# Forty-eight chunks of up to 508 tokens instead of fifty-two of up to 470: chunk ends inside stage D's groups

## The chip, the cores and the metric

The kernel runs on one core of one Trainium2 chip. The metric is the device time of one execution in microseconds (us), the median of several runs. One core has TensorE (PE, matrix products), VectorE (DVE), ScalarE (ACT), GpSimd (POOL) and SyncE (SP, which here only issues the transfers). PE takes its weights with a separate load, PEld in the profile.

## The reference

Eight sequences (batches) of 3008 tokens with 256 numbers each go through a transform, a complex mixing matrix, a threshold and the transform back, and the 24,064 tokens that come out go through two matrices with a squared ReLU between them.

```python
X = np.fft.rfft(x, axis=1)
Yr = Xr @ w_r - Xi @ w_i + b_r
Yi = Xr @ w_i + Xi @ w_r + b_i
Yr = np.sign(Yr) * np.maximum(np.abs(Yr) - lam, 0.0)     # Yi alike
y = np.fft.irfft(Y, n=3008, axis=1)
h = np.maximum(y.reshape(24064, 256) @ w_in, 0.0)        # w_in 256 x 2048
return h * h @ w_out                                     # w_out 2048 x 256
```

## The kernel before, in words

**The transform** splits 3008 = 47 x 64. Stage A takes the 47-point part, 64 columns in 13 groups (`GROUPS`: twelve of 5 columns, one of 4). Stage B takes the 64-point part, the mixing, the threshold and the 64-point part back, in 12 pairs of rows (`NPAIR`). Stage D takes the 47-point part back, again in the 13 groups; a group of 5 columns gives 5 x 47 = 235 tokens, the group of 4 gives 188. Between the stages the data go through scratch in HBM (`s1`, `s2`): `store_a` and `load_b`, `store_c` and `load_d`. Nearly every product is done on a high and a low part of each operand, three matmuls each (`mm3`, lines 205 to 207).

**The two matrices** work on chunks of tokens. Before, a chunk is two neighbouring groups of stage D, so it has 470 tokens (48 chunks) or, where the two groups of 4 columns meet at a batch's border, 376 (4 chunks): 52 chunks. Batches with odd numbers begin with their group of 4 columns for this (`groups_of`). A chunk takes 8 rounds (`NU`), 416 rounds in all and 2 more to drain. A round has:

- `mm1`: 12 matmuls of the chunk's full width (470) into `ph`, tokens `xt` by weights `wi`;
- `squares` on ACT (L839 twice, L840): ReLU and square into `g`; `sums` on DVE (L846 to L848): three more combinations of halves, so that seven products of half width do the work of eight;
- one round later the split of `g`: `gh` on ACT (L889) and `gl` on DVE (L897), 7 x 236 = 1652 columns each;
- two rounds later `mm2`: 7 products of three matmuls, 21 of half width (236), into four banks `po`.

After a chunk's last round `put_together` (L864 to L876) adds the products on DVE and issues four stores to `outT`.

**The order is written out by hand.** `plan` holds for each round what of stages A, B and D is issued at fixed places in it: "load" (SP, at the start), "a1" and "a2" (ACT, behind `gh`, and at the end), "p1" (PE, between `mm1` and `mm2`), "p2" (PE, behind `mm2`), "v1" (DVE, behind `gl`, ahead of `sums`) and "v2" (DVE, at the end). Each engine runs its instructions in this order. Call r0 the first round of a batch's stage B. Its pair i is spread over rounds from r0 + 3i: points `psb` at p2 of that round, `psm` (18 matmuls, the mixing) at p1 two rounds on, `psc` at p1 seven rounds on. Stage A's group i has its load in round r0 - 17 + i, its fold (L233, L234, DVE v1) two rounds on, `psa` (6 matmuls, p2) one more on, its store `eva` one or none more on. Stage D's group has its load two rounds ahead of its points `psd` (p1), and the tokens go to `xt` one round on. Batches 0 and 1 do stage A, and batch 0 all, in `start`, ahead of the rounds; so stage B runs in the rounds for batches 1 to 7 and stage A for 2 to 7.

`stage_b` puts r0 of batch 1 at round 2 and each later one 36 + 15 = 51 rounds on, so that stage A of the next batch lies in the 15 rounds between two stages B. Stage D's two groups for a chunk take the last two free rounds (`pair_round`: while stage B runs, only every third) ahead of the chunk.

**Buffers that the change or the steps below touch:** `ps_f`, two PSUM banks that `psa`, `psb`, `psm1`, `psm2`, `psc` and `psd` take in turn; `ld`, two buffers for loads of stages A and B (`xin`, `bin`); `din`, one buffer for loads of stage D; `ev`, two buffers for what goes back to scratch (`eva`, `evc`); `xt`, two chunks of tokens; `ft`, one buffer, used by stage A's fold and by stage B's threshold; `p1`, `o0`, `o1` of `put_together`; `xl` and `z` of stage B.

Of the kernel before, what the change touches and what calls it, by code (L numbers as in the profile page):

```python
# [28 lines left out]
F32 = mybir.dt.float32  # L29
# [15 lines left out]
W = 5  # L45
GROUPS = [(g, min(W, N2 - g)) for g in range(0, N2, W)]
# [118 lines left out]
def fft_mix_moe(ctx: ExitStack, tc: tile.TileContext, xp, xu, w_r, w_i, b_r, b_i,  # L165
                w_in, w_out, t_u, t_a, t_b, t_b0, t_m, t_d, sgn, outT):
    nc = tc.nc
    B = xp.shape[0] + xu.shape[0]
# [85 lines left out]
    def add_e(e, p1, p2):  # L254
        e = e.rearrange("p (c e) -> p c e", c=2)
        nc.vector.tensor_add(e, p1[:, None, 0:D].broadcast_to([P, 2, D]), bias2)
# [11 lines left out]
    def load_d(c, u, t):  # L268
        b, g, w = chunks[c][u]
        nc.sync.dma_start(out=t[:NR * w], in_=scr2[b][:, g:g + w, :])  # L270
# [13 lines left out]
    def unfold(c, u, ps, v, xf):  # L284
        w = chunks[c][u][2]
        n, m = NR * w, N1 * w
        nc.vector.tensor_add(xf[:, :, :n], ps[:, :, 0], v[:, :, :n])
        nc.vector.tensor_sub(xf[:, :, n:m], ps[:, :, 0, w:], v[:, :, w:n])

    def part_x(c, u, xt):  # L290
        m = N1 * chunks[c][u][2]
        base = N1 * sum(w for _, _, w in chunks[c][:u])
        return m, [x[:, :, base:base + m] for x in xt]

    def start():

        with ExitStack() as own:
# [186 lines left out]
            xs, pm, zs, pc, got = {}, {}, {}, {}, {}  # L484
# [50 lines left out]
                copy(i, ev, pc.pop(i))  # L535
                store_c(0, i, ev)

            def inverse(c, xt):
                got = [tl("xl", bufs=2, name="din") for _ in chunks[c]]
                for u, t in enumerate(got):  # L540
                    load_d(c, u, t)
                yield
                for u, t in enumerate(got):
                    ps = points_d(c, u, t, pst("psd"))
                    v = tl("t", name="dv")[:, :2 * NR * W].rearrange("p (k m) -> p k m", k=2)
                    xf = tl("z", name="dx")[:, :2 * N1 * W].rearrange("p (k m) -> p k m", k=2)
                    m, (hi, lo) = part_x(c, u, xt)
                    nc.scalar.copy(v[:, :, :ps.shape[3]], ps[:, :, 1])
                    unfold(c, u, ps, v, xf)
# [16 lines left out]
            xt = alloc_x(0)  # L566
            late = tables_main()
            for n in range(NPAIR + 3):
# [35 lines left out]
    xts = {0: start()}  # L604
# [20 lines left out]
    def at(r, place, do):  # L625
        plan.setdefault((r, place), []).append(do)
# [50 lines left out]
    def plan_b(b, r0):  # L677
        for i in range(NPAIR):
            def steps(i=i):
                s = {}  # L680
# [32 lines left out]
                    add_e(s["e"], *s["p"])  # L713

                def threshold():
                    t = tl("ft", name="t")
                    nc.vector.tensor_scalar(t, s["e"], LAM, -LAM, op0=ALU.min, op1=ALU.max)
                    nc.vector.tensor_sub(s["e"], s["e"], t)

# [27 lines left out]
                r = r0 + PAIR * i  # L747
# [14 lines left out]

            steps()

    def plan_d(c, u, r):
        s = {}

        def load():
            if c not in xts:
                xts[c] = alloc_x(c)  # L770
            s["t"] = tl("din")
            load_d(c, u, s["t"])

        def points():
            s["ps"] = points_d(c, u, s["t"], pst("psd"))

        def take():
            s["v"] = tl("xh", (P, 3, 2, P), name="dv").rearrange("p a b m -> p (a b m)")
            s["v"] = s["v"][:, :2 * NR * W].rearrange("p (k m) -> p k m", k=2)
            nc.scalar.copy(s["v"][:, :, :s["ps"].shape[3]], s["ps"][:, :, 1])  # L780

        def unfolded():
            s["x"] = tl("xl", (P, 3, 2, P), name="dx").rearrange("p a b m -> p (a b m)")
            s["x"] = s["x"][:, :2 * N1 * W].rearrange("p (k m) -> p k m", k=2)
            unfold(c, u, s["ps"], s["v"], s["x"])

        def high():
            m, (hi, lo) = part_x(c, u, xts[c])
            nc.scalar.copy(hi, s["x"][:, :, :m])

        def low():
            m, (hi, lo) = part_x(c, u, xts[c])
            nc.vector.tensor_sub(lo, s["x"][:, :, :m], hi.bitcast(F32))  # L793
# [64 lines left out]
    def put_together(c, po):  # L858
        n = cols[c]
        m, t0 = halves(n)  # L860
        p = {s: po[bank][:, half * m:half * m + m] for s, bank, half in PLACES}
        p1 = tl("p1", (P, HALF))[:, :m]
        o = [tl(f"o{k}", (P, 2, HALF))[:, :, :m] for k in range(2)]
        nc.scalar.copy(p1, p[0])  # L864
        add, sub = nc.vector.tensor_add, nc.vector.tensor_sub
        add(o[0][:, 0], p[2], p1)
# [4 lines left out]
        add(o[0][:, 1], p[3], o[0][:, 1])  # L871
        sub(o[1][:, 0], o[1][:, 0], p[1])
        for k in range(2):
            for t, (a, b) in enumerate(((0, t0), (0, m))):
                to = col0[c] + t * t0
                nc.sync.dma_start(out=outT[k * P:(k + 1) * P, to:to + b - a], in_=o[k][:, t, a:b])  # L876
# [4 lines left out]
    with tc.manual_schedule():  # L881
        for r in range(last + LAG):
            c, j = divmod(r, NU)
            run(r, "load")
            k = r - 1
            if k in hid:
                m, _ = halves(cols[k // NU])
# [6 lines left out]
            if r < last:  # L894
                g = squares(c, ph)
# [7 lines left out]
            k = r - LAG  # L903
# [48 lines left out]
```

## Time and profile before

| | us |
|---|---|
| median of 3 runs | 2704.31 (2702.66 to 2705.11) |
| the profiled execution, its own time | 2704.11 |
| its span in the trace | 2702.3 |
| PE busy | 2624.7 (97% of the span) |
| PE weight loads busy | 2425.5 (90%) |
| DVE busy | 2147.3 (79%) |
| ACT busy | 2031.8 (75%) |
| mean granted TensorE clock | 0.99 |

The page counts a matmul as busy from its start to its modelled end, and neighbours overlap, so PE's busy share is no measure of its pace; the distance between two starts in the timeline is. In a row of a group of instructions stand line, engine, operation, output<-input, shapes, count, then busy us and mean ns of one, then the idle time of the engine ahead of them and who ended it. In a row of the timeline stand start in us, duration in us, engine, line, operation, and in brackets the idle time ahead of it. SPq is SP's issuing of transfers.

### The profile page before, as it was taken

How to read it: one execution, taken by the hardware profiler on the slowest of the kernel's cores; microseconds unless marked ns; L12 is line 12 of the kernel's file. 1: busy time of each engine (PE TensorE's matmuls, PEld its weight loads, DVE VectorE, ACT ScalarE, POOL GpSimd, SP SyncE). 2: the span in 40 equal slices, each digit the busy share in tenths (PEclk: the TensorE clock that was granted, in tenths of full speed). 3: DMA queues.
4: the chain of work that ended last, by engine and by line, in shares of the span. 5: the costliest groups of instructions: out<-in, count | busy, mean ns of one | idle time of the engine just before them, and what ended most of it. 6: DMA issues, size and time to landing. Idle time of an engine off the chain costs nothing.

```text
span 2702.3 us, 44970 instructions
## 1 busy us (share of the span) xinstructions
PE 2624.7 (97%) x17816; PEld 2425.5 (90%) x17816; DVE 2147.3 (79%) x3301; ACT 2031.8 (75%) x2885; POOL 51.3 (2%) x60
## 2 busy tenths in 40 slices
PE   7889999999999999999999999999999999999998
PEld 4579999999899999999989999999999999999997
DVE  4768888788788888888888888878888888777776
ACT  3668787787777778778777877878877787766765
POOL 1410000000000000000000000000000000000000
PEclk8989999999999999999999999999999999999999
DMA  8611113111221112211132112311123121000000
GB/s 253 192 47 53 44 49 101 51 43 54 67 84 49 39 43 85 79 39 52 46 92 62 49 37 60 99 54 47 39 75 94 35 57 35 27 28 25 19 26 19
DMA packets 130068, 165.33 MB, mean 61 GB/s; under 512 B 11440, under 2 KB 92066, under 8 KB 129666
## 3 DMA queue, kind: packets, MB, share of 16 engines
q1 hardware_dynamic: 129858, 162.44, 20.2%
q8 instruction: 142, 2.33, 0.4%
q14 instruction: 68, 0.56, 0.1%
HBM read 87.43 MB, written 74.97 MB: 60 GB/s over the span
## 4 chain that ended last, share of the span: by engine, by line
PE 47%; DVE 26%; ACT 19%; issue 5%; DMA 2%; POOL 1%; SPq 0%; ACTq 0%; DVEq 0%; POOLq 0%
ACT gh L889 10%; DVE gl L897 7%; PE ph L205 6%; PE ph L206 6%; PE ph L207 6%; PE po L207 6%; PE po L206 6%; PE po L205 6%; DVE g L846 4%; ACT g L840 3%; ACT g L839 3%; DVE g L847 3%; DVE g L848 2%; PE psm L207 2%; PE psb L242 2%
## 5 line engine op out<-in xcount | busy, mean ns | idle before, releaser
L897 DVE TENSOR_TENSOR gl<-g,gh 128x1652 fp32r<-128x1652 f32 (+1 forms) x416 | 770.4, 1852 | 345.1 <-ACT gh L889 345.1
L889 ACT CAST gh<-g 128x1652 fp32r<-128x1652 f32 (+1 forms) x416 | 645.9, 1553 | 401.2 <-DVE g L848 320.9
L205 PE MATMUL po<-gh,wo 128*128 128x236 f32 (+1 forms) x2912 | 809.4, 278 | 5.1 <-DVE o L871 1.8
L206 PE MATMUL po<-gl,wo 128*128 128x236 f32 (+1 forms) x2912 | 799.2, 274 | 2.4 <-DVE gl L897 2.4
L207 PE MATMUL po<-gh,wo 128*128 128x236 f32 (+1 forms) x2912 | 799.9, 275 | 0.0
L205 PE MATMUL ph<-xt,wi 128*128 128x470 f32 (+1 forms) x1664 | 634.9, 382 | 16.9 <-ACT xt L199 10.5
L206 PE MATMUL ph<-xt,wi 128*128 128x470 f32 (+1 forms) x1664 | 624.5, 375 | 4.0 <-DVE xt L793 3.7
L207 PE MATMUL ph<-xt,wi 128*128 128x470 f32 (+1 forms) x1664 | 619.2, 372 | 0.0
L205 PEld LDWEIGHTS po<-gh,wo 128*128 128x128 f32 x2912 | 555.3, 191 | 19.1 <-DVE o L871 5.9
L206 PEld LDWEIGHTS po<-gl,wo 128*128 128x128 f32 x2912 | 554.7, 190 | 8.9 <-DVE gl L897 2.8
L207 PEld LDWEIGHTS po<-gh,wo 128*128 128x128 f32 x2912 | 556.4, 191 | 0.0
L839 ACT ACTIVATE g<-ph 128x472 f32<-128x472 f32 (+1 forms) x832 | 417.6, 555 | 66.7 <-PE ph L207 66.5
L840 ACT ACTIVATE g<-g 128x944 f32<-128x944 f32 (+1 forms) x416 | 408.9, 983 | 13.2
L205 PEld LDWEIGHTS ph<-xt,wi 128*128 128x128 f32 x1664 | 315.7, 190 | 52.6 <-ACT xt L199 10.7
L207 PEld LDWEIGHTS ph<-xt,wi 128*128 128x128 f32 x1664 | 314.5, 189 | 39.5
L206 PEld LDWEIGHTS ph<-xt,wi 128*128 128x128 f32 x1664 | 316.6, 190 | 34.8 <-DVE xt L793 6.8
L846 DVE TENSOR_TENSOR g<-g 128x472 f32<-128x472 f32 (+1 forms) x416 | 266.4, 640 | 38.0 <-ACT g L840 26.2
L848 DVE TENSOR_TENSOR g<-g 128x236 f32<-128x236 f32 (+1 forms) x416 | 166.6, 400 | 14.4
L847 DVE TENSOR_TENSOR g<-g 128x236 f32<-128x236 f32 (+1 forms) x416 | 166.5, 400 | 14.3
L207 PE MATMUL psm<-wm,xl 128*128 128x256 f32 (+1 forms) x552 | 162.0, 293 | 4.5 <-DVE xl L702 3.8
L205 PE MATMUL psm<-wm,xh 128*128 128x256 f32 (+1 forms) x552 | 160.9, 291 | 0.0
L206 PE MATMUL psm<-wm,xh 128*128 128x256 f32 (+1 forms) x552 | 159.3, 289 | 0.0
(107 smaller groups left out, 2771.1 us busy)
## 6 DMA issues: line engine op xcount, KB each, us to landing
bin<-s SPq DMA_DIRECT2D x96, 256.0 KB
s<-evc SPq DMA_DIRECT2D x96, 256.0 KB
din<-s SPq DMA_DIRECT2D x96, 240.0 KB
xin<-in_xp_dram SPq DMA_DIRECT2D x72, 240.0 KB
s<-eva SPq DMA_DIRECT2D x72, 240.0 KB
outT_dram<-o SPq DMA_DIRECT2D x96, 118.0 KB
outT_dram<-o SPq DMA_DIRECT2D x96, 117.0 KB
s<-eva SPq DMA_DIRECT2D x22, 192.0 KB
```

The source lines that it names most:

```text
L205: nc.tensor.matmul(out, l0, r0, start=start, stop=False, **kw)
L206: nc.tensor.matmul(out, l0, r1, start=False, stop=False, **kw)
L207: nc.tensor.matmul(out, l1, r0, start=False, stop=stop, **kw)
L242: nc.tensor.matmul(ps[:, k, :, q, :], tv[:, q, k], tB[:, 0:r + 2:r + 1], start=True, stop=True)
L839: nc.scalar.activation(g[:, t:4:2, :m], ph[:, :, t * t0:t * t0 + m], AF.Relu)
L840: nc.scalar.activation(g[:, 0:4, :m], g[:, 0:4, :m], AF.Square)
L846: nc.vector.tensor_sub(g[:, 4:6, :m], g[:, 1:4:2, :m], g[:, 0:2, :m])
L847: nc.vector.tensor_sub(g[:, 6, :m], g[:, 3, :m], g[:, 4, :m])
L848: nc.vector.tensor_sub(g[:, 1, :m], g[:, 6, :m], g[:, 2, :m])
L889: nc.scalar.copy(gg[k][0][:, :, :m], hid[k][:, :, :m])
L897: nc.vector.tensor_sub(gg[k][1][:, :, :m], hid.pop(k)[:, :, :m], gg[k][0][:, :, :m].bitcast(F32))
```

## The change

A batch now has six chunks of 470, 508, 508, 508, 508 and 506 tokens (`WIDTHS`), 48 chunks and 384 rounds in all. `mm1` is up to 508 wide, `mm2` up to 254, `gh` and `gl` 7 x 254 = 1778. All batches take the groups in the same order. Chunk ends lie inside four of a batch's 13 groups: such a group writes its first tokens to the current `xt` as before (round r + 1), and the others, which belong to the chunk after it, stay in `o0`'s buffer until the current chunk's matmuls begin: in that round the `xt` of the chunk before comes free, and they are copied there. These are four more casts on ACT and four more subtractions on DVE in each batch. Stage D's first load of a batch waits for the round `done`, one earlier after the last pair than before. `stage_b` starts at round 3 and repeats every 48 rounds, so the 15 rounds of stage A begin in round r0 + 33 of the batch before. The threshold's scratch is now in `z`, and `p1` in `o1`.

```diff
-def groups_of(b):
-    return GROUPS if b % 2 == 0 else GROUPS[-1:] + GROUPS[:-1]
+WIDTHS = (2 * W * N1, 508, 508, 508, 508, 506)
+NCH = len(WIDTHS)
...
-    HALF = (W * N1 + 1) // 2 * 2
-    NCOL = 2 * W * N1
+    NCOL = max(WIDTHS)
+    HALF = (NCOL // 2 + 1) // 2 * 2
...
-    chunks = [flat[i:i + 2] for i in range(0, len(flat), 2)]
-    cols = [N1 * sum(w for _, _, w in ch) for ch in chunks]
+    nch = NCH * B
+    cols = [WIDTHS[c % NCH] for c in range(nch)]
+    col0 = [sum(cols[:c]) for c in range(nch)]
+    def pieces(b, i):
+        g, w = GROUPS[i]
+        a, z = b * S + N1 * g, b * S + N1 * (g + w)
+        out = []
+        for c in range(NCH * b, NCH * (b + 1)):
+            lo, hi = max(a, col0[c]), min(z, col0[c] + cols[c])
+            if lo < hi:
+                out.append((c, lo - col0[c], hi - lo, lo - a))
+        return out
...
                 def threshold():
-                    t = tl("ft", name="t")
+                    t = tl("z", name="t")
...
         def unfolded():
-            s["x"] = tl("xl", (P, 3, 2, P), name="dx").rearrange("p a b m -> p (a b m)")
+            if len(parts) == 1:
+                x = tl("xl", (P, 3, 2, P), name="dx").rearrange("p a b m -> p (a b m)")
+            else:
+                x = tl("o0", (P, 2, HALF), name="dx").rearrange("p a m -> p (a m)")
...
-        at(r - 2, "load", load)
+        at(max(r - 2, done.get(b, 0)), "load", load)
...
-        at(r + 1, "a1", high)
-        at(r + 1, "v1", low)
+        for k, part in enumerate(parts):
+            q = NU * (part[0] - 1) if k else r + 1
+            at(q, "a1", lambda part=part: high(*part))
+            at(q, "v1", lambda part=part: low(*part))
...
-    stage_b = {1: 2}
-    for b in range(2, B):
-        stage_b[b] = stage_b[b - 1] + PAIR * NPAIR + TURN
-    done = {b: r + PAIR * (NPAIR - 1) + 9 for b, r in stage_b.items()}
+    stage_b = {b: 3 + NU * NCH * (b - 1) for b in range(1, B)}
+    done = {b: r + PAIR * (NPAIR - 1) + 8 for b, r in stage_b.items()}
...
-        for u in (1, 0):
-            r = rounds.pop()
+        units = [i for i in range(len(GROUPS)) if pieces(b, i)[0][0] == c]
+        for i, r in zip(units, rounds[-len(units):]):
...
-        p1 = tl("p1", (P, HALF))[:, :m]
         o = [tl(f"o{k}", (P, 2, HALF))[:, :, :m] for k in range(2)]
+        p1 = o[1][:, 0]
```

Two places show what moves. The first is DVE in round r0 + 35 of batch 2, in which the last pair's mixing is biased. Before, from that pair's `zl` on (names: `e<-psm` takes a mixing bank and frees it, `g` are the sums, `gl` opens the next round):

```order
L735 TENSOR_TENSOR zl<-z,zh 128x512
L846 TENSOR_TENSOR g<-g 128x472
L847 TENSOR_TENSOR g<-g 128x236
L848 TENSOR_TENSOR g<-g 128x236
L256 TENSOR_TENSOR e<-psm_7118,bias_68 128x512
L257 TENSOR_TENSOR e<-psm_7119,e 128x512
L897 TENSOR_TENSOR gl<-g,gh 128x1652
```

and now:

```order
L741 TENSOR_TENSOR zl<-z,zh 128x512
L233 TENSOR_TENSOR f<-xin 120x256
L234 TENSOR_TENSOR f<-xin 120x256
L858 TENSOR_TENSOR g<-g 128x508
L859 TENSOR_TENSOR g<-g 128x254
L860 TENSOR_TENSOR g<-g 128x254
L256 TENSOR_TENSOR e<-psm_7092,bias_68 128x512
L257 TENSOR_TENSOR e<-psm_7093,e 128x512
L659 TENSOR_TENSOR fl<-f,fh 120x512
L909 TENSOR_TENSOR gl<-g,gh 128x1778
```

The next batch's folds `f` now stand ahead of the sums and of the two adds that free the mixing banks, and its `fl` behind them; every width of the two matrices' work is larger.

The second place is SP at the border from batch 2 to 3, from the last stores of stage A (`eva`) to the first loads of stage B (`bin`). Before:

```order
L270 DMA din<-s_2_4635 120x1x512
L226 DMA s_3_7034<-eva 24x5x512
L270 DMA din<-s_2_4635 120x1x512
L226 DMA s_3_7034<-eva 24x5x512 x3
L226 DMA s_3_7034<-eva 24x4x512
L222 DMA bin<-s_3_7034 128x2x256 x2
L270 DMA din<-s_2_4635 120x1x512
```

and now:

```order
L280 DMA din<-s_2_4555 120x1x512
L226 DMA s_3_6771<-eva 24x5x512
L280 DMA din<-s_2_4555 120x1x512
L226 DMA s_3_6771<-eva 24x5x512
L226 DMA s_3_6771<-eva 24x4x512
L888 DMA outT_dram<-o_7932 128x252
L888 DMA outT_dram<-o_7932 128x254
L888 DMA outT_dram<-o_7933 128x252
L888 DMA outT_dram<-o_7933 128x254
L222 DMA bin<-s_3_6771 128x2x256 x2
L280 DMA din<-s_2_4555 120x1x512
```

Four output stores now stand between the last `eva` and the first `bin`, and a second `din`, which needs the points of the first one done, stands ahead of the last two `eva` instead of the last four.

More of the change, by code (lines that the diff above doesn't have):

```diff
@@ L57 @@
 F_MAX = _f32(0x47EFFFFF)
-def groups_of(b):
-    return GROUPS if b % 2 == 0 else GROUPS[-1:] + GROUPS[:-1]
+WIDTHS = (2 * W * N1, 508, 508, 508, 508, 506)
+NCH = len(WIDTHS)
 def token_order(b):
     n1 = np.r_[np.arange(NR), N1 - np.arange(1, NR)]
-    return np.concatenate([((64 * n1[:, None] + 47 * (g + np.arange(w))) % S).reshape(-1) for g, w in groups_of(b)])
+    return np.concatenate([((64 * n1[:, None] + 47 * (g + np.arange(w))) % S).reshape(-1) for g, w in GROUPS])
 def folded_rows():
@@ L257, in add_e, with load_d, points_d @@
         nc.vector.tensor_add(e, p2.rearrange("p (c e) -> p c e", c=2), e)
-    flat = [(b, g, w) for b in range(B) for g, w in groups_of(b)]
-    chunks = [flat[i:i + 2] for i in range(0, len(flat), 2)]
-    cols = [N1 * sum(w for _, _, w in ch) for ch in chunks]
-    col0 = [sum(cols[:c]) for c in range(len(chunks))]
-    nch = len(chunks)
+    nch = NCH * B
+    cols = [WIDTHS[c % NCH] for c in range(nch)]
+    col0 = [sum(cols[:c]) for c in range(nch)]
+    assert sum(WIDTHS) == S
+    def pieces(b, i):
[7 more added lines that the diff above has]
+        return out
     def alloc_x(c):
         return [const.tile([P, 2, NCOL], F32R, tag=f"xt{k}", name=f"xt{k}", bufs=2) for k in range(2)]
-    def load_d(c, u, t):
-        b, g, w = chunks[c][u]
+    def load_d(b, i, t):
+        g, w = GROUPS[i]
         nc.sync.dma_start(out=t[:NR * w], in_=scr2[b][:, g:g + w, :])
-    def points_d(c, u, t, ps):
-        b, g, w = chunks[c][u]
+    def points_d(i, t, ps):
+        g, w = GROUPS[i]
         n = NR * w
@@ L282, in points_d, with unfold @@
         return ps
-    def unfold(c, u, ps, v, xf):
-        w = chunks[c][u][2]
+    def unfold(i, ps, v, xf):
+        w = GROUPS[i][1]
         n, m = NR * w, N1 * w
@@ L288, in unfold @@
         nc.vector.tensor_sub(xf[:, :, n:m], ps[:, :, 0, w:], v[:, :, w:n])
[L290 to L293, printed above, removed]
     def start():
@@ L536, in pair_out, with inverse @@
                 store_c(0, i, ev)
-            def inverse(c, xt):
-                got = [tl("xl", bufs=2, name="din") for _ in chunks[c]]
+            def inverse(xt):
+                got = [tl("xl", bufs=2, name="din") for _ in range(2)]
                 for u, t in enumerate(got):
-                    load_d(c, u, t)
+                    load_d(0, u, t)
                 yield
                 for u, t in enumerate(got):
-                    ps = points_d(c, u, t, pst("psd"))
+                    ps = points_d(u, t, pst("psd"))
                     v = tl("t", name="dv")[:, :2 * NR * W].rearrange("p (k m) -> p k m", k=2)
                     xf = tl("z", name="dx")[:, :2 * N1 * W].rearrange("p (k m) -> p k m", k=2)
-                    m, (hi, lo) = part_x(c, u, xt)
+                    (_, base, m, _), = pieces(0, u)
+                    hi, lo = (x[:, :, base:base + m] for x in xt)
                     nc.scalar.copy(v[:, :, :ps.shape[3]], ps[:, :, 1])
-                    unfold(c, u, ps, v, xf)
+                    unfold(u, ps, v, xf)
                     split(xf[:, :, :m], hi, lo)
@@ L591, in start @@
                     weights()
-            inv = inverse(0, xt)
+            inv = inverse(xt)
             next(inv)
@@ L763, in plan_b, with plan_d @@
             steps()
-    def plan_d(c, u, r):
+    def plan_d(b, i, r):
         s = {}
+        parts = pieces(b, i)
         def load():
-            if c not in xts:
-                xts[c] = alloc_x(c)
             s["t"] = tl("din")
-            load_d(c, u, s["t"])
+            load_d(b, i, s["t"])
         def points():
-            s["ps"] = points_d(c, u, s["t"], pst("psd"))
+            s["ps"] = points_d(i, s["t"], pst("psd"))
         def take():
@@ L782, in unfolded, with high, low @@
         def unfolded():
-            s["x"] = tl("xl", (P, 3, 2, P), name="dx").rearrange("p a b m -> p (a b m)")
[L784 to L793, printed above, removed]
-        at(r - 2, "load", load)
+            if len(parts) == 1:
+                x = tl("xl", (P, 3, 2, P), name="dx").rearrange("p a b m -> p (a b m)")
+            else:
+                x = tl("o0", (P, 2, HALF), name="dx").rearrange("p a m -> p (a m)")
+            s["x"] = x[:, :2 * N1 * W].rearrange("p (k m) -> p k m", k=2)
+            unfold(i, s["ps"], s["v"], s["x"])
+        def high(c, to, m, a):
+            if c not in xts:
+                xts[c] = alloc_x(c)
+            nc.scalar.copy(xts[c][0][:, :, to:to + m], s["x"][:, :, a:a + m])
+        def low(c, to, m, a):
+            hi, lo = (x[:, :, to:to + m] for x in xts[c])
+            nc.vector.tensor_sub(lo, s["x"][:, :, a:a + m], hi.bitcast(F32))
+        at(max(r - 2, done.get(b, 0)), "load", load)
         at(r, "p1", points)
@@ L816, in fft_mix_moe @@
     for c in range(1, nch):
-        rounds = [r for r in range(NU * (c - 1) + 1, NU * c - 1) if pair_round(r)]
-        for u in (1, 0):
-            r = rounds.pop()
-            assert r - 2 >= done.get(chunks[c][u][0], 0) - 2 and r >= 2, (c, u, r)
-            plan_d(c, u, r)
+        b = c // NCH
+        rounds = [r for r in range(max(NU * (c - 1) - 1, 2), NU * c - 1) if pair_round(r)]
+        units = [i for i in range(len(GROUPS)) if pieces(b, i)[0][0] == c]
+        for i, r in zip(units, rounds[-len(units):]):
+            assert r - 1 >= done.get(b, 0), (c, i, r)
+            assert len(pieces(b, i)) == 1 or r >= NU * (c - 1) + 2, (c, i, r)
+            plan_d(b, i, r)
     def mm1(c, j):
```

1 line of the change is left out of this document (removed).

## The prediction

> **What bounds the kernel now.** I read the page's shares first, then the timeline of PE where stage B runs, then the groups by form, then the waits.
>
> ```profile
> PE 2624.7 (97%) x17816; PEld 2425.5 (90%) x17816; DVE 2147.3 (79%) x3301; ACT 2031.8 (75%) x2885; POOL 51.3 (2%) x60
> ```
>
> PE is the fullest engine, but its share says nothing of its pace. The timeline of PE does (start, duration, line, operation); here is the first matmul of each run of one kind, over one round and a half:
>
> ```profile
> 1507.09 0.39 PE L205 MATMUL psc<-zh,tMs 128*128 128x512 f32 x1
> ...
> 1507.78 0.27 PE L205 MATMUL po<-gh,wo 128*128 128x236 f32 x1
> ...
> 1510.13 0.37 PE L205 MATMUL ph<-xt,wi 128*128 128x470 f32 x1
> ...
> 1512.68 0.28 PE L205 MATMUL psm<-wm,xh 128*128 128x256 f32 x1
> ...
> 1514.71 0.28 PE L205 MATMUL po<-gh,wo 128*128 128x236 f32 x1
> ...
> 1517.06 0.38 PE L205 MATMUL ph<-xt,wi 128*128 128x470 f32 x1
> ```
>
> The kernel issues 3 `psc`, 21 `po`, 12 `ph` and 18 `psm` in these runs, so the distances are 0.69/3 = 0.230 us at 512 columns, 2.35/21 = 0.112 at 236, 2.55/12 = 0.2125 at 470 and 2.03/18 = 0.113 at 256. Run follows run without a hole: PE's issue is the bound here. The distances do not grow with the width below 256. A round of a 376 chunk shows it more clearly:
>
> ```profile
> 484.79 0.33 PE L206 MATMUL ph<-xt,wi 128*128 128x376 f32 x1
> ...
> 486.66 0.25 PE L205 MATMUL po<-gh,wo 128*128 128x188 f32 x1
> ...
> 488.98 0.36 PE L205 MATMUL ph<-xt,wi 128*128 128x376 f32 x1
> ```
>
> Eleven `ph` take 1.87, 0.170 each; 21 `po` of 188 columns take 2.32, 0.1105 each, as much as 236 columns. The groups by form say the same of thousands (the mean ns follows the bar):
>
> ```profile
> L205 PE MATMUL po<-gh,wo 128*128 128x236 f32 x2688 | 747.5, 278 | 4.2 <-DVE o L871 1.4 <-DVE o L866 1.1 <-ACT gh L889 0.8
> L206 PE MATMUL ph<-xt,wi 128*128 128x470 f32 x1536 | 581.7, 379 | 3.5 <-DVE xt L793 3.3
> L205 PE MATMUL po<-gh,wo 128*128 128x188 f32 x224 | 61.9, 276 | 0.9 <-DVE o L871 0.4 <-DVE o L866 0.3
> L206 PE MATMUL ph<-xt,wi 128*128 128x376 f32 x128 | 42.8, 334 | 0.4 <-DVE xt L793 0.4
> ```
>
> So `mm1` pays for columns, `mm2` pays by the matmul. The kernel pays 52 x 8 x 21 = 8736 of the latter, and the idle time ahead of these groups is a few us in all.
>
> **The change part by part.** *Fewer, wider matmuls.* A round of a 470 chunk costs PE 12 x 0.2125 + 21 x 0.112 = 4.90, one of a 376 chunk 12 x 0.170 + 21 x 0.1105 = 4.36; before, 384 x 4.90 + 32 x 4.36 = 2021. The new widths have no row, so I bound them. `ph` at 508: the line through 470 and 512 gives 0.2283, the one through 376 and 470 gives 0.2297; I take 0.229. `po` at 254: one neighbour is `psm` at 256 with 0.113, the other is `psa`, also at 256:
>
> ```profile
> 749.15 0.28 PE L205 MATMUL psa<-fh,tAs 120*120 120x256 f32 x1
> ...
> 749.74 0.28 PE L207 MATMUL psa<-fh,tAs 120*120 120x256 f32 x1
> ```
>
> Five steps in 0.59, 0.118 each; less two columns, 0.117. The line through `ph` at 376 and 470, drawn down to 254, gives 0.115, in the middle, and I take that: columns begin to count where they take longer than the floor of 0.111. A new round is then 12 x 0.229 + 21 x 0.115 = 5.16, and 64 x 4.90 + 320 x 5.16 = 1965: **-56**. With `po` at 0.1125 and `ph` at 0.2283 it would be -75, with 0.117 and 0.2297 it would be -39. The matmuls of stages A, B and D keep their number.
>
> *The two element engines.* DVE's part of a round grows as well:
>
> ```profile
> L897 DVE TENSOR_TENSOR gl<-g,gh 128x1652 fp32r<-128x1652 f32 x384 | 721.4, 1879 | 317.6 <-ACT gh L889 317.6
> L846 DVE TENSOR_TENSOR g<-g 128x472 f32<-128x472 f32 x384 | 248.9, 648 | 33.7 <-ACT g L840 23.0
> L848 DVE TENSOR_TENSOR g<-g 128x236 f32<-128x236 f32 x384 | 155.2, 404 | 13.2
> L897 DVE TENSOR_TENSOR gl<-g,gh 128x1316 fp32r<-128x1316 f32 x32 | 48.9, 1529 | 27.5 <-ACT gh L889 27.5
> ```
>
> It is now 1.879 + 0.648 + 2 x 0.404 = 3.34 (L847 as L848); the two forms of `gl` differ by 350 ns over 336 columns, 1.04 ns a column, so 254 wide it is 2.01 + 0.685 + 2 x 0.423 = 3.54. That is 0.20 more in a round in which PE gets 0.26 more: the balance stays, and `gl`'s 317.6 us of waiting for ACT show that DVE has room. The 32 extra casts and 32 extra subtractions of the split groups lie in that room: 0.
>
> *Stage A over the end of stage B.* This is the new place, rounds r0 + 33 to r0 + 36, at six borders. DVE there:
>
> ```profile
> L702 DVE TENSOR_TENSOR xl<-x,xh 128x768 fp32r<-128x768 f32 x84 | 79.9, 952 | 0.0
> L793 DVE TENSOR_TENSOR xt<-dx,xt 128x470 fp32r<-128x470 f32 x94 | 60.5, 643 | 0.0
> L718 DVE TENSOR_TENSOR e<-e,t 128x512 f32<-128x512 f32 x84 | 58.2, 692 | 2.9
> L735 DVE TENSOR_TENSOR zl<-z,zh 128x512 fp32r<-128x512 f32 x84 | 57.5, 685 | 0.0
> L256 DVE TENSOR_TENSOR e<-psm,bias 128x512 f32<-128x512 f32 x84 | 57.4, 684 | 0.0
> L653 DVE TENSOR_TENSOR fl<-f,fh 120x512 fp32r<-120x512 f32 x72 | 49.4, 686 | 10.6 <-ACT fh L649 10.4
> L287 DVE TENSOR_TENSOR dx<-psd,dv 128x240 f32<-128x240 f32 x96 | 38.9, 405 | 50.2 <-ACT dv L780 48.5 <-ACT dv L548 1.7
> L717 DVE TENSOR_SCALAR t<-e 128x512 f32<-128x512 f32 x84 | 35.3, 421 | 0.0
> L250 DVE TENSOR_TENSOR x<-x 128x256 f32<-128x256 f32 x84 | 35.2, 419 | 0.0
> L233 DVE TENSOR_TENSOR f<-xin 120x256 f32<-120x256 f32 x72 | 30.2, 419 | 0.2
> ```
>
> Four rounds at 3.54 are 14.2; two thresholds 2 x 1.11, one sum and low part 1.37, one `zl` 0.69, two biased adds 1.37, one unfolded group with its low part 1.4, four folds with theirs 4 x 1.52 = 6.1: 27.4 in all. PE has 4 x 5.16, `psd` and `psb` (8 each at 0.112) 1.8, `psc` 0.7, `psm` 2.0, three `psa` 2.1: 27.2. So DVE is level with PE for four rounds, and what it was late by is not hidden. One wait is new: in r0 + 35 `psa` needs the bank that the first biased add frees. In the round shown above that add was
>
> ```profile
> 1516.62 0.68 DVE L256 TENSOR_TENSOR e<-psm,bias 128x512 f32<-128x512 f32 x1
> ```
>
> so it ended at 1517.30, 0.24 after PE had gone on to the next round at 1517.06. A fold of 0.84 ahead of it makes that 1.1 us, and `psa` stands in PE's order ahead of the next `mm1`, so all of PE waits. With half as much again for late low parts I take 1.5 us a border, 6 x 1.5 = **+9**; bounds 0 (DVE comes in early) and 4 us a border.
>
> *SP at the border.* The first `bin` needs the last `eva` landed; four output stores now stand between.
>
> ```profile
> 465.94 0.88 SPq L876 DMA_DIRECT2D outT_dram<-o  x2
> ...
> 476.42 1.58 SPq L226 DMA_DIRECT2D s<-eva  x2
> ...
> 480.76 4.41 SPq L222 DMA_DIRECT2D bin<-s  x3
> ...
> 483.65 1.13 PE L242 MATMUL psb<-tB,bin 128*128 128x128 f32 x8 [0.54 <-DVE dx L287]
> ```
>
> Here SP had issued the last `eva` at 478.0 and waited for it until 480.76. Four stores at 0.44 are 1.8 and fit into these 2.8, so `bin` leaves no later. I count 0.3 us a border for their traffic, **+2** (bounds -5 to +12, as the rivals explain). Stage D's first load one round nearer to its points costs 0: `bin` above was used 2.9 us after its issue, and a round is over 5.
>
> *Four `put_together` fewer*, each seven adds of 0.4 on DVE of which PE loses a part: **-2** (0 to -4). `p1` in `o1` and the threshold in `z` find their buffers long free: 0.
>
> The sum: -56 + 9 + 2 - 2 = -47, on 2704.1 of the profiled execution (span 2702.3 and 1.8 around it), which stands 0.2 under the median of the runs: **2657**.
>
> **The rivals.** *The floor still covers 254 columns* (`psm`'s 0.113 speaks for it; `psa`'s 0.118 and the line of `ph` against): -75 + 9 = **2638**. The Trainium skill, TensorE: Matmul & The Clock Gate, sections "LDWEIGHTS (loading the stationary operand)" and "Back-to-back issue gap", would side with it: it has a weight load take columns/1.2 ns, 106.7 for 128, and a warm matmul N/2.4 + 2.5, 108.3 for 254. By its figures alone, an estimate, the matmuls' sum would be -61; the trace has 0.2125 at 470 where that rule has 0.198, so its slope is not this kernel's.
>
> *DVE binds at the borders.* With DVE level with PE, folds that wait for their `xin` (the second one now waits on SP for the last `psb` to free its buffer) make every delay PE's: 5 us a border instead of 1.5, +21, **2678** to 2690. For it speak the sums above, against it that DVE idles for 317.6 us of `gl` alone and enters the border with slack.
>
> *Slower: SP blocked at both ends of a border.* Two groups of stage D in neighbouring rounds share the one `din`: the second load stops SP until the first group's points, and stores behind it keep `ev`. Once, before, that reached PE:
>
> ```profile
> 735.78 0.78 SPq L270 DMA_DIRECT2D din<-s  x1
> ...
> 740.51 0.58 ACT L744 COPY evc<-psc 128x512 f32<-128x512 f32 x1 [4.02 <-DMA s<-eva]
> ...
> 741.14 0.57 PE L205 MATMUL psa<-fh,tAs 120*120 120x256 f32 x1 [3.05 <-ACT evc L744]
> 741.51 0.41 PE L206 MATMUL psa<-fl,tAs 120*120 120x256 f32 x1
> 741.72 0.41 PE L207 MATMUL psa<-fh,tAs 120*120 120x256 f32 x1
> ```
>
> PE lost 3.05 us, and after it ran `psa` at 0.21 instead of 0.118, so some 5 us. Each border now has two such pairs, so at worst 10 to 11 us a border: -58 + 66, **2712**. It decides from 10.5 us a border on. Against it: the other such pair shown above (478 to 484) cost PE 0.54, and `evc` now leaves SP ahead of both `din`. If the one old stall vanishes, that is the -5 in the bounds.
>
> **How the numbers follow.** My forecast 0.62 (its own range 2645 to 2675), the covered floor 0.17, DVE at the borders 0.13, SP 0.04, something unseen 0.04. The range 2634 to 2692 leaves out the SP case and the ends of the others. Over 0.2% (5.4 us, about what a measurement tells from no change) faster: 0.92, within it 0.03, slower 0.05.
>
> **What would show it.** In the profile after: 8064 `po` at about 0.115 between starts and `ph` near 0.229; in rounds r0 + 35 a `psa` waiting about 1 us for DVE's biased add; `bin` issued when the last `eva` has landed. I am wrong if `po` at 254 goes at 0.112 or 0.118, if PE waits over 3 us at a border, or if rounds away from the borders show waits that they did not have.

## The result and the profile after

| | before | after |
|---|---|---|
| median, us | 2703.48 (2700.08 to 2705.11, 4 runs) | 2671.36 (2670.41 to 2673.4, 4 runs) |
| profiled execution, its own time | 2704.11 | 2671.44 |
| its span | 2702.3 | 2669.7 |

The ratio is 0.9885, with a 95% interval of 0.9873 to 0.9898: 32 us less, where 47 were forecast.

The page's shares after (engine, busy us, share of the span, instructions) have PE at 97% as before:

```profile
PE 2583.5 (97%) x16760; PEld 2328.8 (87%) x16760; DVE 2123.1 (80%) x3177; ACT 2014.2 (75%) x2785; POOL 50.9 (2%) x60
```

So again the timeline has to tell the pace. Here is the first matmul of each run of one kind, over two rounds and a half of the kernel after:

```profile
1518.12 0.39 PE L205 MATMUL psc<-zh,tMs 128*128 128x512 f32 x1
...
1518.82 0.28 PE L205 MATMUL po<-gh,wo 128*128 128x254 f32 x1
...
1521.30 0.39 PE L205 MATMUL ph<-xt,wi 128*128 128x508 f32 x1
...
1524.05 0.28 PE L205 MATMUL psm<-wm,xh 128*128 128x256 f32 x1
1526.10 0.28 PE L205 MATMUL po<-gh,wo 128*128 128x254 f32 x1
...
1528.60 0.39 PE L205 MATMUL ph<-xt,wi 128*128 128x508 f32 x1
...
1531.35 0.28 PE L205 MATMUL po<-gh,wo 128*128 128x254 f32 x1
```

Twelve `ph` take 2.75, 0.229 each, as forecast. Twenty-one `po` take 2.48 and 2.50: 0.118 and 0.119 each, where 0.115 was taken and 0.117 was the upper bound.

What PE waited for, by the view of the waits (releaser, us in total, times, longest). Before:

```profile
PE psb L242 <- DMA bin<-s: 16.6, 2, 15.3
...
PE psa L205 <- ACT evc L744: 3.0, 1, 3.0
PE psd L280 <- DMA din<-s: 2.6, 2, 2.4
```

After:

```profile
PE psb L242 <- DMA bin<-s: 19.2, 3, 15.6
PE psd L290 <- DMA din<-s: 11.5, 7, 3.3
...
PE psm L205 <- ACT eva L670: 2.3, 6, 0.4
...
PE psa L205 <- DVE e L256: 1.6, 6, 0.3
```

(In both, the longest wait of `psb` for `bin` and of `psd` for `din` is one at the start, ahead of the rounds.) All rows of this view add to 70.7 us before and to 78.9 after. Three waits are new. One is the forecast one, `psa` for the biased add, once a border; it is 0.3 instead of 1.1. The `psm` just ahead of it waits as well. And `psd` waits for `din` at the borders, which the prediction had put at 0. `psb` waits once at each border too; the view puts four of these six waits down to DVE's sums (3.7 us in all), but they go with the others in `e5_start` below. One border in the timeline, where the four waits shown add to 3.4 us:

```profile
399.75 0.38 PE L205 MATMUL psm<-wm,xh 128*128 128x256 f32 x1 [0.42 <-ACT eva L670]
...
404.19 0.38 PE L205 MATMUL psa<-fh,tAs 120*120 120x256 f32 x1 [0.26 <-DVE e L256]
...
448.42 1.15 PE L290 MATMUL psd<-tD,din 120*128 120x120 f32 x8 [1.52 <-DMA din<-s]
...
489.86 1.13 PE L242 MATMUL psb<-tB,bin 128*128 128x128 f32 x8 [1.19 <-DMA bin<-s]
```

### The profile page after: what moved, and what is told of

Same layout as the page of the kernel before. It is cut to its first block, busy times and chain, and to the rows that moved or that the text cites. A ratio compares the mean times of both kernels' runs of the same rounds, so it can differ in the third digit from the quotient of the medians.

```text
span 2669.7 us, 42564 instructions
## 1 busy us (share of the span) xinstructions
PE 2583.5 (97%) x16760; PEld 2328.8 (87%) x16760; DVE 2123.1 (80%) x3177; ACT 2014.2 (75%) x2785; POOL 50.9 (2%) x60
## 4 chain that ended last, share of the span: by engine, by line
PE 61%; DVE 19%; ACT 12%; DMA 4%; issue 3%; POOL 1%; ACTq 0%; SPq 0%; DVEq 0%; POOLq 0%
PE ph L205 8%; PE ph L206 8%; PE ph L207 8%; PE po L205 7%; PE po L207 7%; PE po L206 7%; ACT gh L901 6%; DVE gl L909 5%; DVE g L858 3%; PE psb L242 3%; PE psm L207 2%; PE psd L290 2%; PE psm L205 2%; PE psm L206 2%; ACT g L852 2%
## 5 line engine op out<-in xcount | busy, mean ns | idle before, releaser
L909 DVE TENSOR_TENSOR gl<-g,gh 128x1778 fp32r<-128x1778 f32 (+1 forms) x384 | 763.6, 1989 | 332.9 <-ACT gh L901 332.9
L901 ACT CAST gh<-g 128x1778 fp32r<-128x1778 f32 (+1 forms) x384 | 638.7, 1663 | 381.7 <-DVE g L860 305.8
L205 PE MATMUL po<-gh,wo 128*128 128x254 f32 (+1 forms) x2688 | 764.8, 285 | 6.4 <-DVE o L878 3.6
L206 PE MATMUL po<-gl,wo 128*128 128x254 f32 (+1 forms) x2688 | 753.0, 280 | 2.6 <-DVE gl L909 2.6
L207 PE MATMUL po<-gh,wo 128*128 128x254 f32 (+1 forms) x2688 | 752.9, 280 | 0.0
L205 PE MATMUL ph<-xt,wi 128*128 128x508 f32 (+2 forms) x1536 | 608.6, 396 | 16.2 <-ACT xt L199 10.6
L206 PE MATMUL ph<-xt,wi 128*128 128x508 f32 (+2 forms) x1536 | 599.9, 391 | 1.8 <-DVE xt L802 1.7
L207 PE MATMUL ph<-xt,wi 128*128 128x508 f32 (+2 forms) x1536 | 599.0, 390 | 0.0
L205 PEld LDWEIGHTS po<-gh,wo 128*128 128x128 f32 x2688 | 509.4, 190 | 21.1 <-DVE o L878 7.7
L207 PEld LDWEIGHTS po<-gh,wo 128*128 128x128 f32 x2688 | 510.4, 190 | 0.0
L851 ACT ACTIVATE g<-ph 128x508 f32<-128x508 f32 (+1 forms) x768 | 410.4, 588 | 68.9 <-PE ph L207 67.7
L852 ACT ACTIVATE g<-g 128x1016 f32<-128x1016 f32 (+1 forms) x384 | 401.5, 1046 | 12.2
L858 DVE TENSOR_TENSOR g<-g 128x508 f32<-128x508 f32 (+1 forms) x384 | 260.7, 679 | 46.1 <-ACT g L852 39.4
L859 DVE TENSOR_TENSOR g<-g 128x254 f32<-128x254 f32 (+1 forms) x384 | 161.6, 421 | 13.2
L860 DVE TENSOR_TENSOR g<-g 128x254 f32<-128x254 f32 (+1 forms) x384 | 161.5, 421 | 13.2
```

The costliest lines, as they stand in the source:

```text
L205: nc.tensor.matmul(out, l0, r0, start=start, stop=False, **kw)
L206: nc.tensor.matmul(out, l0, r1, start=False, stop=False, **kw)
L207: nc.tensor.matmul(out, l1, r0, start=False, stop=stop, **kw)
L851: nc.scalar.activation(g[:, t:4:2, :m], ph[:, :, t * t0:t * t0 + m], AF.Relu)
L852: nc.scalar.activation(g[:, 0:4, :m], g[:, 0:4, :m], AF.Square)
L858: nc.vector.tensor_sub(g[:, 4:6, :m], g[:, 1:4:2, :m], g[:, 0:2, :m])
```

## The experiments

All but `e8_overlap` are edits of the kernel after. Times are set against it by the ratios of both to the kernel before, which ran beside each on the same chip; a ratio is uncertain by about 0.0013, 3.5 us, and a difference of two by about 5.

**The width alone (`e1_narrow`, `e2_ladder`).**

```diff
+        n = m if j == 0 or m < 254 else 240     # e2: 250, 246, 242, 238, 230 by chunk
-            mm3(po[bank][:, half * m:half * m + m], ... (gg[0][:, s, :m], gg[1][:, s, :m]), ...
+            mm3(po[bank][:, half * m:half * m + n], ... (gg[0][:, s, :n], gg[1][:, s, :n]), ...
```

> In every second-layer step but the first of a chunk, the matmuls into po of the 508 chunks take 240 of their 254 columns; the products of the other 14 columns are left out in seven of eight rounds. All else is as in the changed kernel. In its trace po of 254 columns stands 0.1185 us from the next, po of 236 before stood at 0.112. Theory A: beyond the floor the columns are paid for, and 254 is beyond it. 320 rounds x 7/8 x 21 = 5880 matmuls each go back by 0.0065: -38 us, so 2633. Theory B: the spacing rose for something else in the new rounds (more operands in flight, DVE's or ACT's traffic), not for the width: within 5 us of 2671. In between, the width explains that share of 38.

> One look at the curve. The second-layer matmuls of the six chunks of a batch take 236 (the 470 chunk, unchanged), 250, 246, 242, 238 and 230 columns in seven of eight steps; the remaining columns' products are left out there. Theory A (a floor of about 0.112 us, and above it the columns at the slope of the ph rows, some 0.45 ns each): 250 at 0.117, 246 at 0.115, 242 at 0.113, 238 and 230 at 0.112, so the knee lies near 240. Theory B (the floor reaches past 250 and something else slows the 254 round): one value for all widths. Theory C (no floor, all linear): 230 at 0.108 and falling by 0.0018 per four columns.

Measured: `e2_ladder` 2657.2 in its one run. Its timeline, first `po` of a run and the first matmul behind the run, at 250, 242, 238 and 230 columns:

```profile
559.29 0.28 PE L205 MATMUL po<-gh,wo 128*128 128x250 f32 x1
...
561.74 0.39 PE L205 MATMUL ph<-xt,wi 128*128 128x508 f32 x1
...
651.77 0.27 PE L205 MATMUL po<-gh,wo 128*128 128x242 f32 x1
...
654.14 0.39 PE L205 MATMUL ph<-xt,wi 128*128 128x508 f32 x1
...
699.52 0.27 PE L205 MATMUL po<-gh,wo 128*128 128x238 f32 x1
...
701.88 0.39 PE L205 MATMUL ph<-xt,wi 128*128 128x508 f32 x1
...
754.43 0.27 PE L205 MATMUL po<-gh,wo 128*128 128x230 f32 x1
...
756.77 0.28 PE L205 MATMUL psa<-fh,tAs 120*120 120x256 f32 x1
```

By 21 that is 0.1167, 0.1129, 0.1124 and 0.1114 (246 columns lie between, at 0.1152). Theory A holds: a floor of 0.112 up to about 240 columns, and above it some 0.45 ns for each column, the slope of `ph`. Width alone explains the 0.1185 at 254.

`e1_narrow` has its `po` at 0.1125, as expected, which is 35 us less of issue. But it took 2655.69 (2651.34 to 2663.27), ratio 0.9823 (0.9808 to 0.9839): only 17 less. By what was expected, the missing half would be something other than the width; but the distances show that the width gave all 35. Half of it was lost again somewhere else.

**Where the other half went (`e12_light`, `e13_elem`).** `e12_light` narrows ACT's and DVE's work on the same columns as well (relu, square, sums, `gh`, `gl`); `e13_elem` narrows theirs and nearly leaves PE's: its `po` take 252 columns in two stretches of 126, partly from another operand's columns.

```diff
+    def part(c, j):
+        m, t0 = halves(cols[c])
+        return (m if j == 0 or m < 254 else 240), t0
-        m, t0 = halves(cols[c])                # squares; sums, gh and gl alike
+        m, t0 = part(c, j)
```

> As e1_narrow, but ACT's and DVE's work on these columns (relu, square, the sums, the high and the low part) takes 240 of 254 columns too in seven of eight steps; the same products are left out. In e1_narrow po fell from 0.1185 to 0.1125 us, 5880 x 0.006 = 35 us, but the time fell by 16 only, and waits of PE for DVE and ACT rose. Theory A (that half was lost to the element engines, which set the pace of a round as soon as PE's part gets shorter): with 5.5% less work there the rest comes back, 2671 - 35 = 2636. Theory B (lost to the holes at the borders and the clock, not to the element engines): 2652 to 2658, as e1_narrow.

> The counterpart of e1_narrow: ACT's and DVE's work of seven of eight steps takes 240 of 254 columns, as in e12_light, but the second-layer matmuls take 252 columns, as two stretches of 126 (half of them another operand's, so the products are not the reference's there). PE's part is then that of the changed kernel less 5880 x 0.0009 = 5 us. The prediction counted the element engines' growth at 0. Theory A (they cost PE time in the changed kernel already): the stalls of PE, 74 us there, fall to about the 57 of e12_light, so 2671 - 5 - 15 = 2651. Theory B (they cost only once PE's part is shortened): 2664 to 2668.

Measured: `e12_light` 2624.59 (2623.78 to 2624.93), ratio 0.9711 (0.9697 to 0.9724), 47 less than the kernel after. `e13_elem` 2649.38 (2644.05 to 2649.85), ratio 0.979 (0.9777 to 0.9804), 26 less, although its `po` still stand at 0.118. Theory A holds in both, and in `e12_light` more strongly than expected. The traces say where the time went. Take PE's distances from start to start, from the first `ph` on, and count each matmul at the mean distance of its kind and width (distances over 1.3 times the median left out of the mean); the rest is time in which PE stood still or ran at the slow clock:

| us | matmuls at their own distances | the rest |
|---|---|---|
| before | 2481.6 | 68.0 |
| after | 2447.9 | 72.2 |
| `e1_narrow` (its slowest execution) | 2414.2 | 95.2 |
| `e12_light` | 2414.2 | 57.9 |
| `e13_elem` | 2450.6 | 41.5 |
| `e7_seven`, below | 2558.0 | 40.6 |

So `e13_elem` gains nothing on the matmuls and 31 us on the rest, with DVE only 41 us less busy and ACT 43 (2% of each): most of what these engines save becomes time, almost as much as the whole change had brought. Both share figures (DVE 80%, ACT 75%) hide this. The groups of the kernel after show how (busy us, mean ns, then idle time ahead and its releasers):

```profile
L909 DVE TENSOR_TENSOR gl<-g,gh 128x1778 fp32r<-128x1778 f32 x320 | 643.4, 2011 | 277.1 <-ACT gh L901 277.1
...
L901 ACT CAST gh<-g 128x1778 fp32r<-128x1778 f32 x320 | 537.8, 1681 | 304.5 <-DVE g L860 243.6 <-PE po L207 32.0 <-DVE e L256 27.0
...
L851 ACT ACTIVATE g<-ph 128x508 f32<-128x508 f32 x640 | 345.2, 593 | 51.3 <-PE ph L207 50.2
...
L852 ACT ACTIVATE g<-g 128x1016 f32<-128x1016 f32 x320 | 337.7, 1055 | 10.2
```

`gh` waits for DVE's last sum 0.76 us a round (243.6/320), `gl` for `gh` 0.87. ACT has 2 x 0.593 + 1.055 + 1.681 = 3.92 us of work in a round and 0.95 of waiting ahead of `gh`: 4.87 of the 5.24 that PE's round takes, before any copy of stages A, B and D. The two engines take turns on one operand, and the idle time of each within the turn is the other's work. It is no room. (That the time is lost in this turn is a reading of these rows; the runs show that their work costs PE time, and no run takes the turn apart.)

**Seven chunks (`e7_seven`).**

```diff
-WIDTHS = (2 * W * N1, 508, 508, 508, 508, 506)
+WIDTHS = (2 * W * N1, 424, 424, 424, 422, 422, 422)
```

> The changed kernel with seven chunks for each batch (470, three of 424, three of 422 columns): 448 rounds instead of 384. Theory A (second-layer matmuls below some 240 columns cost their floor, the first layer's go by columns): a 424 round is 12 x 0.192 + 21 x 0.1115 = 4.65, 384 x 4.65 + 64 x 4.92 = 2099 against 1990: +109, so about 2780, or 75 over the kernel before. Theory B (the time goes with columns alone, and what the change saved was something else, such as fewer borders of chunks): within 15 us of 2671.

Measured: 2752.13 (2749.38 to 2754.95), ratio 1.0181 (1.0167 to 1.0194): 80 more than the kernel after. Its timeline, one round:

```profile
577.68 0.37 PE L205 MATMUL ph<-xt,wi 128*128 128x424 f32 x1
580.01 0.28 PE L205 MATMUL psm<-wm,xh 128*128 128x256 f32 x1
...
582.06 0.26 PE L205 MATMUL po<-gh,wo 128*128 128x212 f32 x1
...
584.39 0.37 PE L205 MATMUL ph<-xt,wi 128*128 128x424 f32 x1
```

2.33/12 = 0.194 and 2.33/21 = 0.111: the issue grows as theory A says. Against that, the waits of PE get shorter, which fits the two runs above (the element engines' work shrinks with the width, the floor does not): by the table above the matmuls take 110 us more than in the kernel after, and the rest is 41 us instead of 72. Theory B is out.

**Stage A over the end of stage B (`e8_overlap`).** The kernel before with this step of the change:

```diff
-                    t = tl("ft", name="t")
+                    t = tl("z", name="t")
-        stage_b[b] = stage_b[b - 1] + PAIR * NPAIR + TURN
+        stage_b[b] = stage_b[b - 1] + PAIR * NPAIR + 12
```

> The kernel before with its 52 chunks; only stage A of the next batch runs over the end of stage B, as in the changed kernel (and the threshold's scratch tile is the other one). This is the term +9 of the prediction alone, without new widths. The prediction: +9 (0 to 24 at most), 2711. Rival: what stage A gives up in waiting rounds it gains by coming earlier, and the fall of the clock once per execution behind the old stall goes: 0 to -6, 2698 to 2704.

Measured: 2706.92 (2703.45 to 2709.07, 11 runs), ratio 1.0016 (1.0007 to 1.0025): 4 more, 2 to 7 by the interval. The sign is the prediction's, the size half of it. Its waits have the same two rows that are new in the kernel after:

```profile
PE psm L205 <- ACT eva L664: 2.9, 6, 0.5
...
PE psa L205 <- DVE e L256: 1.4, 6, 0.2
```

But the 4 us are a balance. The old stall of `psa` for `evc`, which the prediction priced at some 5 us with the slow clock behind it, is gone from this list too, so what the step costs may be nearer to 9. Nor is the overlap the only thing that moved: stages B begin 48 rounds apart instead of 51, so the last `psb` starts at 2199.3 instead of 2296.0, and `psc` waits 5.6 us for `dx` instead of 3.4. No run separates these.

**The biased add ahead of the sums (`e4_bias`).**

```diff
-                at(r + 2, "v2", biased)
+                at(r + 2, "v2" if i + 1 < NPAIR else "v1", biased)
```

> Only the last pair's two biased adds are put ahead of the round's sums on DVE instead of behind them. Theory A (the step of the prediction: psa in round r0 + 35 waits some 1.2 us for the bank that the first biased add frees): 6 x 1.2 = 7 less, 2664. Theory B (the sums, which free po, then come late by as much and PE waits there): within 3 us of 2671, with the wait moved from psa to po. It would be slower by up to 5 if gl and the next low parts follow late too.

Measured: 2669.3 (2666.83 to 2673.1), ratio 0.988 (0.9866 to 0.9895): 1 less, not to be told from nothing. The wait of `psa` for `e` is gone from the list, and no row of `po` took its place. That wait was 1.6 us in all, so theory A's 7 was too much for it; the waits of `psm` for `eva`, 2.3 us, stay as they were. Seven less lies just outside what was measured, 1 less give or take 5; a gain of 1.6 cannot be told from theory B's nothing.

**Stage D's places at the border (`e3_border`, `e5_start`, `e9_front`).** `e3_border` ends stage B one or two rounds sooner and spreads the border's five groups of stage D. `e5_start` only spreads the last three of them. `e9_front` is `e3_border` with the loads of `din` ahead of the round's `xin` on SP, the first one two rounds ahead.

```diff
+                z, o = (5, 7) if i + 1 < NPAIR else (4, 5)      # e3, e9: zhigh, zlow at r + z, back, out at r + o
-    done = {b: r + PAIR * (NPAIR - 1) + 8 for b, r in stage_b.items()}
+    done = {b: r + PAIR * (NPAIR - 1) + 6 for b, r in stage_b.items()}     # e3, e9
+        spread = {0: (-4, -2), 1: (0, 2, 6)}.get(c % NCH) if b else None     # e5: 1 alone
+        take = [NU * NCH * b + d for d in spread] if spread else rounds[-len(units):]
...
-        at(max(r - 2, done.get(b, 0)), "load", load)
+        plan.setdefault((max(r - lead, done.get(b, 0)), "load"), []).insert(0, load)     # e9; e3, e5: at(...)
```

> Only the end of stage B and stage D's places at a border change: the last pair's z, back product and output stores come one and two rounds sooner, and the five groups of stage D around a border stand at rounds -4, -2, 0, +2 and +6 of the new batch, with their loads one round ahead, so that no two share neighbouring rounds. Theory A (SP is blocked by the one din at both ends of a border, and PE waits for it: 1.8 us in the round -3 for din, 1.1 us in round r0 for bin): 6 x 2.9 = 17 less, of which 2 to 5 may come back where the new places crowd, so -12 to -17, about 2657. Theory B (those waits stand in for others that are due at the same place, the element engines' backlog): within 5 us of 2671.

> Only the three groups of stage D at the beginning of a batch move: from neighbouring rounds to rounds 0, +2 and +6, with their loads one round ahead. The end of stage B and the two groups ahead of the border stay as in the changed kernel. Theory A (SP, held by the one din, issues the first bin late, and PE waits for it in round r0): about 9 less over the kernel, as between the changed kernel and the run e3_border at that place, so 2662. Theory B (bin was late for the last eva's landing, whatever SP does before): within 3 us of 2671. If spreading the groups moves the wait to din, psd waits where psb did, and nothing is gained either.

> The places of the run e3_border, but a border group's load of din is issued ahead of the round's xin on SP, and the first group's load two rounds ahead. In e3_border that load went out only after an xin that waited for DVE, and PE stood for 2.8 us at psd in each batch's round -4, after which the granted clock fell to 0.5 for 3.4 us. Theory A (the place in SP's order did it): the 24 us in round -4 and the 8 in round -2 go, the gains at rounds -3 and r0 (9 each) stay: 2671 - 17 = 2654, and no fall of the clock behind round 0 of a batch. Theory B (din is late because the last evc must land first, with two 240 KB transfers beside it): the wait stays over 2 us, the clock falls six times again, 2680 or more.

Measured: `e3_border` 2690.89 (2686.85 to 2692.06), ratio 0.9956 (0.9944 to 0.9969), 19 slower than the kernel after where 12 to 17 less was expected. `e5_start` 2664.73 (2663.97 to 2667.78), ratio 0.9859 (0.9846 to 0.9873): 7 less, a little over the uncertainty of 5. `e9_front` 2651.44 (2649.95 to 2653.44), ratio 0.9808 (0.9795 to 0.9821): 21 less.

SP's queue in the kernel after, where a batch begins, and in `e5_start`:

```profile
480.53 0.76 SPq L280 DMA_DIRECT2D din<-s  x1
481.40 1.90 SPq L226 DMA_DIRECT2D s<-eva  x2
483.42 1.88 SPq L888 DMA_DIRECT2D outT_dram<-o  x4
486.99 0.89 SPq L222 DMA_DIRECT2D bin<-s  x2
```

```profile
474.56 4.25 SPq L226 DMA_DIRECT2D s<-eva  x2
478.94 3.24 SPq L890 DMA_DIRECT2D outT_dram<-o  x4
482.29 0.93 SPq L222 DMA_DIRECT2D bin<-s  x2
```

Held by `din` until the points of the group before had been read, SP stored the last `eva` late, and the first `bin` needs all of them landed. Without that hold `bin` goes out 4.7 us sooner and the wait of `psb` is gone: theory A of `e5_start`.

In `e3_border` the wait of `psb` went too, but `psd` now waits for `din` twice a border, 26.7 us in all where it was 11.5. SP's queue and PE there, and the clock by stretches of 5 us (PE, PEld, DVE, ACT, POOL busy, then PEclk, the granted clock):

```profile
442.18 0.36 SPq L218 DMA_DIRECT2D xin<-in_xp_dram  x1
442.60 0.78 SPq L280 DMA_DIRECT2D din<-s  x1
```

```profile
446.78 1.55 PE L290 MATMUL psd<-tD,din 120*128 120x120 f32 x8 [2.79 <-DMA din<-s]
```

```profile
440.00:445.00 5.00, 3.99 (x23) 3.18 (x21) 4.20 (x7) 3.82 (x5) 0.00 (x0) 1.00 0.29 61
445.00:450.00 5.00, 3.22 (x17) 3.22 (x18) 4.13 (x6) 2.95 (x5) 0.00 (x0) 0.74 0.38 121
450.00:455.00 5.00, 5.00 (x31) 4.61 (x30) 1.41 (x3) 2.25 (x3) 0.00 (x0) 0.92 0.22 67
```

The load was planned a round ahead, but stood behind an `xin` that waits for DVE's fold, so it was issued in the round that needs it. And the clock fell: (1 - 0.74) x 5 / 0.5 + (1 - 0.92) x 5 / 0.5 = 3.4 us at half speed, at each of the six borders. With the first group's load a round sooner and ahead of `xin` (`e9_front`), it goes out at 431.80 and `psd` runs at 440.96 without a wait; the clock stays whole at all six borders. For the second group only the place in the round's order changed, and its waits, 1.0 to 1.4 us at each border in `e3_border`, are gone as well. The waits of `e9_front` have `psd` for `din` once, at the start, and `psb` for `bin` once, at the start:

```profile
PE psb L242 <- DMA bin<-s: 13.3, 1, 13.3
...
PE psd L290 <- DMA din<-s: 3.8, 1, 3.8
```

**Both border edits (`e11_both`).** `e9_front` and `e4_bias` together.

> The run e9_front with the last pair's biased adds ahead of the sums as in e4_bias: the two border edits together. Theory A (the terms lie at different places and add): e9_front was 2651.4, e4_bias took 2 (0.0005 of 2700 by the ratios): 2649.5. Theory B (with the border clear, the later sums meet PE): 2652 to 2655.

Measured: 2650.79 (2648.8 to 2653.38), ratio 0.9808 (0.9794 to 0.9821), the same as `e9_front`. Nothing is added that can be measured.

So the version that beats both kernels is `e9_front`, 2651.4: the change's own terms, with stage D's loads at the borders where PE no longer waits for them.

## Why the prediction was right, and where it was wrong

*The bound.* Right, but not the whole: PE's issue. Every experiment that changed the width of the matmuls moved their distances as the floor and the slope say.

*Fewer, wider matmuls, -56.* Mis-sized in one term. `ph` at 508 was right. `po` at 254 was "in the middle" of two neighbours at 0.115; it is 0.1185. 320 x 21 x 0.0035 = 23.5 us, so by the prediction's own sum -32. One mistake was in the slope: 0.170 at 376 and 0.2125 at 470 come from one round each. Over all rounds of the kernel before the mean distances are 0.1722 and 0.2143, and the line through these gives 0.1175 at 254, not 0.115. The other was which neighbour to weigh: floor and slope meet near 240 (`e2_ladder`), so 254 already pays for 14 columns, and `psa` at 256 with 0.118 was the right neighbour, `psm` at 256 with 0.113 the wrong one. The rival of a covered floor fell with it.

*The two element engines, 0.* As a difference between the two kernels it cannot be far off, since the rest in the table above rose by only 4 us. But the reason was wrong. The 317.6 us that `gl` waits were read as room; `e13_elem` shows that 2% less busy time of theirs is worth some 26 us in the kernel after, and `e1_narrow` against `e12_light` that they take back half of what a faster PE would win. One row of the page, which the prediction did not use, pointed there: the shares of the chain that ended last. Before:

```profile
PE 47%; DVE 26%; ACT 19%; issue 5%; DMA 2%; POOL 1%; SPq 0%; ACTq 0%; DVEq 0%; POOLq 0%
```

and in `e13_elem`:

```profile
PE 69%; DVE 13%; ACT 9%; DMA 4%; issue 3%; POOL 1%; SPq 0%; ACTq 0%; DVEq 0%; POOLq 0%
```

*Stage A over the end of stage B, +9.* Right in place and sign: `e8_overlap` has +4 (2 to 7), or about 9 if the old stall that it lost is counted as the prediction priced it. The wait named for it was mis-sized: 1.1 us of `psa` is 0.3, and `psm` for the copy of `eva` takes about 0.4.

*SP at the border, +2, and "stage D's first load one round nearer to its points costs 0".* The step that failed. It counted from the round in which the load is planned. SP's queue in the kernel after shows when it goes out:

```profile
444.07 0.34 SPq L218 DMA_DIRECT2D xin<-in_xp_dram  x1
444.51 5.85 SPq L280 DMA_DIRECT2D din<-s  x2
```

An `xin` that waits for DVE's fold stands ahead of it, so it is issued 3.9 us ahead of the points at 448.42, where the prediction had over 5 in hand; the second `din` then holds SP for the rest of the 5.85. `psd` waits 1.5 us at this border, and `psb` 1.2 for `bin`. (The four output stores did fit, as forecast; what came late was the last `eva`, behind `din`.) By `e5_start` the second is worth 7 us, and by `e9_front` against it the first some 14, in which the last pair's earlier end is included. The rival of the blocked SP had the mechanism, both ends of the border and the shared `din`, and put it at 10 to 11 us a border; it is about 3.5.

*The old stall.* The prediction allowed -5 if it vanished. It did: no wait of `psa` for `evc` is in the list after.

The sum with measured terms, from the table and the two profiled executions: -33.7 for the matmuls at their own distances, where -56 was forecast; +4.3 for the rest in the rounds, the overlap, SP and the element engines among it, where +9 was; and -3.6 because the rounds begin at 143.9 us instead of 147.5. With 0.3 at the end that is, but for rounding, the 32.6 by which the span fell. The -3.6 is luck: in the runs of this study the rounds begin between 143.6 and 148.1 whatever the change. So the sign and most of the mechanism were right, and the size was too large by the one term of `po`; the errors in the others were smaller and of both signs.

The prediction's own signs of being wrong were "0.112 or 0.118" for `po`, and it goes at 0.118; and over 3 us of waits at a border, and those shown above add to 3.4. Both came true, although the time lies inside its range.

## What to carry to other kernels

When a matmul is on a floor, find where floor and slope meet before widening it, from rows on both sides and of the same kind. Idle time of an engine that waits for another engine in the same chain is not room; ask what the two together take in a round. And a load's place is not the round it is planned in but what stands ahead of it in its queue, with the waits of those.

## What the runs showed of the hardware

- *Floor and slope.* `po` with 128 x 128 weights: 0.1114 at 230 columns, 0.1124 at 238, 0.1129 at 242, 0.1152 at 246, 0.1167 at 250, 0.1185 at 254.
- *`psm` has two paces.* At 256 columns its runs go at 0.113 or at 0.118, within one kernel, and in the kernel before some begin at 0.118 and change to 0.113 after five matmuls. Why was not found; no experiment was aimed at it.
- *A hole in PE costs more than itself.* In `e3_border` holes of 3.1 to 3.4 us from one matmul's start to the next lowered the granted clock to 0.5 for 3.4 us each time, six of six; so did one of 3.17 in `e1_narrow`. Of the shorter ones in the rounds, one of 2.63 in `e5_start` and one of 2.12 in `e12_light` did so too, while one of 2.74 in the kernel after and one of 2.24 in `e1_narrow` did not; these runs show no threshold. The old stall of the kernel before (3.05 us of idle time) had it as well, and its `psa` ran at 0.21. The Trainium skill, TensorE: Matmul & The Clock Gate, "HAM oscillation — how this bites in real kernels", warns of pauses over about 3.4 us; the length of the fall here agrees with the window of 3.4 us it gives, but the idle parts of these holes, 1.8 to 3.1 us, were shorter than the pauses it warns of.
